# Shared key rests, another query order and earlier turns in a fused attention and FFN kernel

## The chip, the cores and the metric

The kernel runs on one core of a Trainium2 chip. The metric is device time in microseconds (us): the median over several executions. "Span" is the length of one profiled execution, which is some 1.6 to 1.9 us shorter than the time measured around it.

## The reference, cut to what matters

Attention over 8 batches, 12 heads, 448 tokens and 64 dimensions a head; its output, put together over the heads, is the input of a gated FFN.

```python
scores = matmul(q, k.transpose(0, 1, 3, 2)) / sqrt(64)      # q, k, v: (8, 12, 448, 64)
attn_out = matmul(softmax(scores), v)
x = attn_out.transpose(0, 2, 1, 3).reshape(3584, 768)
g = x @ w_gate                                              # 768 x 1536
silu = g * (1 / (1 + exp(-g)))
out = (silu * (x @ w_val)) @ w_out                          # float32, 3584 x 768
```

## The kernel before

Heads are handled in pairs, 48 of them. A pair's scores come in units: a chunk of keys against all 448 queries, both heads side by side in two PSUM banks (one head on rows 0-63 of TensorE, the other on rows 64-127), followed by one exp on ScalarE. Three such "score banks" of two PSUM banks each rotate. The weighted sums need V with a column of ones (so the 65th column gives the softmax's denominator). The result X must be turned, as the FFN needs features on partitions.

The first six pairs are the start. After that the work comes in visits: two or three score units, one pair's weighted sums, then one or two steps of the FFN. The FFN runs in eight blocks of 384 or 512 tokens. A block's gate and value products ("steps") come first, its output products later. Only two small PSUM banks are left for accumulators, value products and output products.

```python
def qk(pr, c):                                  # c: one of 4 chunks of 112 keys
    s = ps_s.tile([128, 2, 512], FP32, tag="s")
    for hx in range(2):
        nc.tensor.matmul(s[:, hx, 0:S], lhsT=t[ts(hx, 64), c * P : c * P + 128],
                         rhs=t[ts(hx, 64), ds(S + (1 - hx) * D, S)], start=True, stop=True)
    nc.scalar.activation(e[:, :, 0:S], s[0:P, :, 0:S], AF.Exp, scale=sm_scale)

def pv_chunk(pr, c):                            # one accumulator bank for both heads
    if c == 0:
        accs[pr] = ps_f.tile([128, 512], FP32, tag="f", name="acc")
    ...                                         # 8 matmuls of 65 columns a chunk

# FFN: gate in a score bank (or a small one), value and output in small banks
gp = ps_s.tile(...) ; group("g", gp) ; tanh on ScalarE
vp = ps_f.tile(...) ; group("v", vp) ; two products on VectorE, into t1 and hts

# loads, by the pair at which they are issued ("g", "v": quarters of the gate and value
# weights, "o": halves of the output weights, "V": values of three pairs)
wq = {
    0: [("qk", 6), ("g", 0), ("v", 0)],
    1: [("V", 2), ("qk", 8, 1), ("g", 1), ("v", 1)],
    3: [("qk", 9, 1), ("qk", 10), ("g", 2), ("v", 2)],
    4: [("g", 3), ("v", 3), ("qk", 12)],
    6: [("V", 3), ("o", 0)],
    7: [("o", 1)],
}
```

q and k of the first 11 pairs are turned by TensorE; later pairs are put in order by GpSimd and turned by a DMA transpose, which I call the key turn below. X of the first 12 pairs is turned by TensorE, that of later pairs by DMA.

The softmax here doesn't subtract the row's maximum and nothing guards it: scores larger than these inputs give would overflow.

## Time and profile before

| | before |
|---|---|
| time, median | 453.26 us |
| span of the profile | 451.7 us |
| first FFN matmul | 29.79 us |
| block 2 starts | 129.86 us |
| last output matmul ends | 446.55 us |
| waits of TensorE after 29.8 us, as listed | 1.2 us |

The prediction, below, shows TensorE's busy shares, a visit of the middle, the start and the tail. Three more views matter for what follows. First the view of waits, TensorE's own, from 30 us on (what waited, for what: us in total, times, longest). There are only four single ones, 1.2 us in all (the two longest shown):

```profile
PE acc L243 <- DVE t L345: 0.4, 1, 0.4
PE rtp L310 <- ACT osb L378: 0.4, 1, 0.4
...
```

Second, from the page: the busy share of the DMA engines in 40 slices of 11.3 us, and the shares of the chain of work that ended last.

```profile
DMA  9999999999969379874749758772503112200033
...
PE 93%; DVE 3%; ACT 2%; issue 1%; DVEq 0%; ACTq 0%
```

### The profile page before, as it was taken

The page shows a single profiled execution, that of the slowest core. Times are in us where ns is not written, and L with a number is a line of the kernel's source. Part 1 is how long each engine was busy: PE and PEld are TensorE (multiplying, and loading weights), DVE is VectorE, ACT ScalarE, POOL GpSimd, SP SyncE. Part 2 cuts the span into 40 slices and gives each one's busy share as a digit, 9 for nine tenths or more (in the row PEclk, how much of TensorE's full clock was granted, in tenths as well). Part 3 has the DMA queues.
Part 4 walks back from the last instruction along what each step waited for, and adds up shares of the span by engine and source line. Part 5 has one row for each costly group of instructions (what it writes and reads, how often), then busy time and mean ns, then how long its engine had stood idle before and what let it go on. Part 6 is the DMA issues. An engine that isn't in the chain of part 4 may idle for free.

```text
span 451.7 us, 9871 instructions
## 1 busy us (share of the span) xinstructions
PE 441.9 (98%) x4024; PEld 247.0 (55%) x4024; DVE 201.6 (45%) x447; ACT 238.8 (53%) x350; POOL 141.8 (31%) x228
## 2 busy tenths in 40 slices
PE   8999999999999999999999999999999999999995
PEld 3655565545455556454555656545455666544563
DVE  3666562456654434455443534353453544055300
ACT  6965666566746465554554546644555462222221
POOL 8755715927642225252313405330100000000000
PEclk9999999999999999999999999999999999999999
DMA  9999999999969379874749758772503112200033
GB/s 142 173 200 201 196 172 174 180 209 119 145 93 133 46 129 124 132 120 71 126 74 120 98 78 143 118 105 68 101 20 68 46 46 57 70 2 0 17 100 95
DMA packets 105101, 48.71 MB, mean 108 GB/s; under 512 B 59744, under 2 KB 101600, under 8 KB 105056
## 3 DMA queue, kind: packets, MB, share of 16 engines
q0 software_dynamic: 43392, 23.37, 41.2%
q1 hardware_dynamic: 61664, 24.71, 28.9%
q8 instruction: 31, 0.51, 0.5%
q14 instruction: 14, 0.11, 0.1%
HBM read 47.19 MB, written 11.01 MB: 129 GB/s over the span
## 4 chain that ended last, share of the span: by engine, by line
PE 93%; DVE 3%; ACT 2%; issue 1%; DVEq 0%; ACTq 0%
PE op L371 24%; PE gp L326 23%; PE vp L326 23%; PE s L217 9%; PE acc L243 9%; PE acc L251 2%; ACT E L225 2%; PE tp L208 1%; PE wp L109 1%; DVE t L345 1%; ACT sg L341 1%; DVE qkT L209 0%; DVE xt L264 0%; PE acc L291 0%; DVE hts L348 0%
## 5 line engine op out<-in xcount | busy, mean ns | idle before, releaser
L225 ACT ACTIVATE E<-s 112x896 f16<-112x896 f32 x192 | 162.1, 919 | 27.5 <-PE s L217 27.4
L326 PE MATMUL gp<-X,wg 128*128 128x384 f16 (+1 forms) x576 | 124.7, 352 | 0.0
L326 PE MATMUL vp<-X,wv 128*128 128x384 f16 (+1 forms) x576 | 124.6, 352 | 0.0
L371 PE MATMUL op<-wo,hts 128*128 128x384 f16 (+1 forms) x684 | 116.1, 323 | 0.0
L345 DVE SCALAR_TENSOR_TENSOR t<-sg,gp 128x384 f32<-128x384 f32 (+1 forms) x96 | 59.7, 621 | 121.8 <-ACT sg L341 121.8
L341 ACT ACTIVATE sg<-gp 128x384 f32<-128x384 f32 (+1 forms) x96 | 52.5, 547 | 84.8 <-PE gp L326 83.6
L371 PEld LDWEIGHTS <-hts 128*128 128x128 f16 x684 | 65.5, 98 | 45.9 <-issue 3.9
L326 PEld LDWEIGHTS <-wv 128*128 128x128 f16 x576 | 56.3, 98 | 52.6
L326 PEld LDWEIGHTS <-wg 128*128 128x128 f16 x576 | 53.1, 97 | 45.6 <-issue 1.1
L378 ACT ACTIVATE osb<-op 128x384 f32<-128x384 f32 (+1 forms) x57 | 27.8, 487 | 92.5 <-PE op L371 92.5
L167 POOL COPY qk<-q 112x512 f16<-112x512 f16 x37 | 22.9, 619 | 144.5 <-DMA qkT<-qk 143.1
L348 DVE SCALAR_TENSOR_TENSOR hts<-t,vp 128x384 f16<-128x384 f32 (+1 forms) x96 | 59.6, 621 | 10.0
L243 PEld LDWEIGHTS <-E 112*128 112x128 f16 x1152 | 46.7, 97 | 18.2 <-issue 17.5
L243 PE MATMUL acc<-vo,E 112*128 112x65 f16 x1152 | 53.0, 193 | 1.3 <-DVE vo L142 0.7
L217 PE MATMUL s<-qkT 64*128 64x448 f16 x384 | 50.6, 355 | 0.2
L251 PE MATMUL acc<-vo,E 112*128 112x65 f16 x384 | 42.9, 193 | 0.0
L262 DVE RECIPROCAL R<-acc 128x7 f32<-128x7 f32 x48 | 9.8, 205 | 70.6 <-PE acc L251 70.5
L129 POOL DMA_DIRECT2D k<-in_k_dram x44 | 29.0, 660 | 9.5 <-DMA wo<-in_moe_w_out_dram 7.8
L129 POOL DMA_DIRECT2D q<-in_q_dram x44 | 29.3, 666 | 5.2 <-PE s L217 2.5
L136 POOL DMA_DIRECT2D vraw<-in_v_dram x42 | 28.0, 666 | 8.4 <-DVE vo L142 7.2
L217 PEld LDWEIGHTS <-qkT 64*128 64x128 f16 x384 | 14.5, 94 | 25.8 <-issue 18.6
L264 DVE TENSOR_TENSOR xt<-acc,R 128x384 f16<-128x384 f32 (+1 forms) x48 | 27.6, 574 | 1.7
(41 smaller groups left out, 148.2 us busy)
## 6 DMA issues: line engine op xcount, KB each, us to landing
q<-in_q_dram POOLq DMA_DIRECT2D x41, 112.0 KB, 4.0
k<-in_k_dram POOLq DMA_DIRECT2D x41, 112.0 KB, 4.6
vraw<-in_v_dram POOLq DMA_DIRECT2D x39, 112.0 KB, 4.6
wg<-in_moe_w_gate_dram POOLq DMA_DIRECT2D x8, 288.0 KB, 10.1
wv<-in_moe_w_val_dram POOLq DMA_DIRECT2D x8, 288.0 KB, 10.2
wo<-in_moe_w_out_dram POOLq DMA_DIRECT2D x2, 1152.0 KB, 22.0
out_dram<-osb SPq DMA_DIRECT2D x8, 288.0 KB, 3.0
out_dram<-osb SPq DMA_DIRECT2D x8, 240.0 KB, 3.1
```

The costliest lines, as they stand in the source:

```text
L129: nc.gpsimd.dma_start(dst[:, ds(h0, 2 * n)], flat.rearrange("h (p c) d -> p h (c d)", c=NC))
L136: nc.gpsimd.dma_start(vraw[:, ds(pr % VS, n)].rearrange("p r h c d -> p (r h) (c d)"), v[b, h : h + 2 * n].rearrange("h (p c) d -> p h (c ...
L217: nc.tensor.matmul(s[:, hx, 0:S], lhsT=t[ts(hx, 64), c * P : c * P + 128], rhs=t[ts(hx, 64), ds(S + (1 - hx) * D, S)], start=True, stop=True,)
L225: nc.scalar.activation(e[:, :, 0:S], s[0:P, :, 0:S], AF.Exp, scale=sm_scale)
L243: nc.tensor.matmul(a7[:, 2 * j + hx], lhsT=e[:, ds(c * EB + 9 * hx + 2 * j, 2)].rearrange("p b x -> p (b x)"), rhs=vo[:, hx, c, 0 : D + 1] ...
L251: nc.tensor.matmul(a7[:, 6], lhsT=e[:, ds(c * EB + 6 + hx, 2)].rearrange("p b x -> p (b x)"), rhs=vo[:, hx, c, 0 : D + 1], start=False, st ...
L326: nc.tensor.matmul(dst[:, 0:n], lhsT=wslice(kind, fb, cb), rhs=X[kk][:, cb, ds(c0, n)], start=(cb == 0), stop=(cb == NCB - 1),)
L341: nc.scalar.activation(sg[:, 0:n], gp[:, 0:n], AF.Tanh, scale=0.5)
L345: nc.vector.scalar_tensor_tensor(t1[:, 0:n], sg[:, 0:n], 1.0, gp[:, 0:n], ALU.add, ALU.mult)
L348: nc.vector.scalar_tensor_tensor(hts[:, fb, 0:n], t1[:, 0:n], 0.5 * HS, vp[:, 0:n], ALU.mult, ALU.mult)
L371: nc.tensor.matmul(op[:, 0:w], lhsT=hts[:, fb, ts(ch, 128)], rhs=wo[oh][:, fb, ds(m0 - oh * OH, w)], start=(fb == 0), stop=(fb == NFB - 1),)
L378: nc.scalar.activation(osb[:, ds(m0, w)], op[:, 0:w], AF.Copy, scale=1.0 / HS)
```

## The change

Its intent: fewer and fuller instructions in attention. Keys come in three chunks of 128 and a rest of 64; the rests of four heads (two pairs) share one score unit on the four 64x64 quarters of the array. That makes 168 units and exps in place of 192. Each head has its own accumulator bank. To make full tiles, queries and keys are loaded in another order (keys and values in two DMAs with a token in common). X of 18 pairs is turned by TensorE, in a score bank. Turns of X go ahead of the next FFN step. The output weights come in four pieces, later than before, and the outputs of block 0 are made in block 1 rather than in block 0.

```diff
-NPE = 11
+NPE = 12
-XPE = 12
+XPE = 18
+START = (
+    "sstssvtsppsppstvsxsvpspppstsppsppsvtsspp"
+    "pvxspsxspppvpstsppxsppsxx"
+)                                  # order of the start: s score, t turn, v copy of V, p sums, x turn of X
...
     def qk(pr, c):
+            ...                    # rest unit: 2 heads x 2 pairs on the four quarters
+            for hx in range(2):
+                for p in (pr, pr + 1):
+                    lo = low(p, hx)
+                    nc.tensor.matmul(
+                        s[ts(1 - lo, 64), hx, 0:S],
+                        lhsT=t[ts(hx, 64), ds(0 if lo else KR * 128 + 64, 64)],
+                        rhs=t[ts(hx, 64), ds(NC * 128, S)], ...
...
-        if c == 0:
-            accs[pr] = ps_f.tile([128, 512], FP32, tag="f", name="acc")
+                accs[pr] = ([fbank(), fbank()], [0, 0])       # a bank a head
...
     def turn_x(pr):
         if pr < XPE:
-            tp = accs[pr] if pr < FIRST else ps_f.tile([128, 512], FP32, tag="f", name="xtp")
+            tp = ps_s.tile([128, 2, 512], FP32, tag="s", name="xtp")[:, 0]
...
-            nc.vector.tensor_copy(dst[:, 0:MQ], tp[:, 0:MQ])
+            nc.vector.tensor_copy(dst, tp[:, 0:S])
-    def turn_rests(b):
-        ...
...                                # output loop: n here overwrites the block's size
-                    c, p0 = divmod((j + D) % S, P)
-                    m = min(P - p0, l0 + 128 - l, (MQ if j < MQ else S) - j)
+                    n = S // NC
+                    c, p0 = divmod(j, n)
+                    m = min(n - p0, l0 + 128 - l)
...
-            1: [("V", 2), ("qk", 8, 1), ("g", 1), ("v", 1)],
-            3: [("qk", 9, 1), ("qk", 10), ("g", 2), ("v", 2)],
-            4: [("g", 3), ("v", 3), ("qk", 12)],
-            6: [("V", 3), ("o", 0)],
-            7: [("o", 1)],
+            1: [("V", 2), ("qk", 8, 1), ("qk", 9, 1), ("g", 1), ("v", 1)],
+            3: [("qk", 10), ("V", 3), ("g", 2), ("v", 2)],
+            4: [("qk", 12), ("g", 3), ("v", 3)],
+            9: [("o", 0), ("o", 1)],
+            11: [("o", 2), ("o", 3)],
...
-            (oq if i == 0 else ffn2_wait).extend(own)
+            ffn2_wait.extend(own)
...
+                for _, p0 in todo:
+                    pv_piece(p0, RU)                          # rest sums straight after the scores
...
+    def run_fv():
+        next(gen)
+        run_turns()                                           # turns of X ahead of later steps
```

## The prediction

> **What bounds the kernel now.** I read the page's busy shares and its row of slices first, then TensorE's order in the steady middle, then the start, then the tail.
>
> The busy shares:
>
> ```profile
> span 451.7 us, 9871 instructions
> PE 441.9 (98%) x4024; PEld 247.0 (55%) x4024; DVE 201.6 (45%) x447; ACT 238.8 (53%) x350; POOL 141.8 (31%) x228
> PE   8999999999999999999999999999999999999995
> ACT  6965666566746465554554546644555462222221
> ```
>
> TensorE (PE) is full in all slices but the first and the last; ScalarE (ACT) has its top value, 9, only in the second. So work that leaves TensorE's order is worth its own length almost everywhere, and work that leaves ScalarE is worth something only in the first 30 us. As ends of matmuls are modelled, I take costs from the start of one group to the start of the next. A visit of the middle (columns: start, length, engine, line, operation, count):
>
> ```profile
> 269.14 0.74 PE L217 MATMUL s<-qkT 64*128 64x448 f16 x6
> 269.82 2.12 PE L371 MATMUL op<-wo,hts 128*128 128x384 f16 x12
> 271.78 1.14 PE L326 MATMUL gp<-X,wg 128*128 128x384 f16 x6
> 272.75 1.14 PE L326 MATMUL vp<-X,wv 128*128 128x384 f16 x6
> 273.82 0.74 PE L217 MATMUL s<-qkT 64*128 64x448 f16 x6
> 274.50 0.36 PE L243 MATMUL acc<-vo,E 112*128 112x65 f16 x6
> ...
> 275.47 0.81 PE L326 MATMUL gp<-X,wg 128*128 128x384 f16 x4
> ```
>
> From the starts: three score units (two heads side by side, 448 columns each) take 274.50 - 273.82 = 0.68 us. A run of two takes 0.48 us (33.78 to 34.26) and a single one 0.29, so a unit is 0.19 us and 0.10 is paid once a run. A group of six FFN matmuls takes 0.97 us before another full-array group (the gate, 271.78 to 272.75) and 1.07 before scores (the value, 272.75 to 273.82). So entering the half-row mode costs 0.10, and leaving it 0.10. A pair's weighted sum, 32 matmuls of 65 columns, takes 275.47 - 274.50 = 0.97 us, 30.5 ns each.
>
> The start, which is ScalarE's: 26 exps run from 6.59 to 29.33, 0.875 us each, nearly unbroken, and the first FFN matmul waits for the sixth pair:
>
> ```profile
> 23.25 6.08 ACT L225 ACTIVATE E<-s 112x896 f16<-112x896 f32 x7 [0.29 <-PE s L217]
> 28.93 0.63 DVE L264 TENSOR_TENSOR xt<-acc,R 128x448 f16<-128x448 f32 x1
> 29.61 0.34 PE L291 MATMUL acc<-ident,xt 128*128 128x128 f16 x3 [0.96 <-DVE xt L264]
> 29.79 1.14 PE L326 MATMUL gp<-X,wg 128*128 128x384 f16 x6
> ```
>
> The tail: TensorE ends near 446.6, one short eviction follows, and then 4.8 us of output transfer and end of program:
>
> ```profile
> 446.59 0.33 ACT L378 ACTIVATE osb<-op 128x192 f32<-128x192 f32 x1 [0.61 <-PE op L371]
> out_dram<-osb SPq DMA_DIRECT2D x10, 192.0 KB, 3.0
> out_dram<-osb SPq DMA_DIRECT2D x12, 48.0 KB, 2.0
> ```
>
> **What the skill says.** The Trainium skill, "TensorEngine Tiling (Array Packing)", section Key Properties: a change of tiling mode drains TensorE, while tiles of one mode load weights and multiply in parallel. The trace agrees on both: 0.10 us a switch, and a score unit of two heads takes 0.19 us, the time of one stream of 448 columns at 2.4 GHz. The same page, Gotcha 1: different row tiles may not write one PSUM bank at a time. That is why the new kernel gives each head its own accumulator; no run yet shows what that costs. "TensorE: Matmul & The Clock Gate", section Wait - 56ns, not 53.3ns?, gives N/2.4 GHz plus about 2.5 ns per matmul: 162.5 ns for 384 columns, and the trace has 0.97/6 = 162 ns.
>
> **The change, part by part.** Counts are from the two built programs, split at the first FFN matmul.
>
> Scores. 448 keys were four chunks of 112; they are now three of 128, and the 64 left over of two heads of two pairs share one unit. Units fall from 192 to 168. The shared unit is four matmuls on the four 64x64 quarters; if all four run together it costs about 0.20 us. After the split: 166 units x 0.187 = 31.0 us before; 124 x 0.187 + 21 x 0.20 = 27.4 after.
>
> Weighted sums. Still 32 matmuls a pair, but 24 use 128 rows and 8 use 64 rows, alternating between the row halves. Pairs of small transposes on different tiles show the likely price: twelve of the present rest-transposes (64 columns) take about 0.21 us without the switch, 17.5 ns each. For 42 pairs after the split: 42 x 0.97 = 40.7 before; 1008 x 30.5 ns + 336 x 17.5 ns = 36.6 after.
>
> Turns. q and k: 3 pairs x 18 x 27.5 ns = 1.5 before; 4 pairs of 8 x 27.5 + 16 x 17.5 ns = 2.0 after (12 pairs are now turned by TensorE, not 11). X: 18 matmuls x 60 ns + 24 rest-transposes x 17.5 = 1.5 before; 36 x 60 + 12 x 30 = 2.5 after (18 pairs, not 12).
>
> Mode switches. 119 before, 132 after: fewer visits (50 against 58), but 21 of the shared units add a step from quarters to halves. At 0.10: 11.9 before, 13.2 after.
>
> FFN. The same columns: 96 x 0.97 + 96 x 1.29 + 56 x 1.95 = 326.1 us in both.
>
> Sum after the split: before 31.0 + 40.7 + 1.5 + 1.5 + 11.9 + 326.1 = 412.7 (the trace has 446.6 - 29.8 = 416.8, so 4 us are waits and small change). After: 27.4 + 36.6 + 2.0 + 2.5 + 13.2 + 326.1 = 407.8. **Gain 4.9 us.**
>
> Start. The sixth pair's sums now need 21 exps, not 24: 3 x 0.875 = 2.6 us earlier. Against it: the first V copy stands ahead of a q/k eviction in VectorE's order, V comes in two issues, and TensorE's own work in the start (some 19 us) is close to ScalarE's 18.4. First FFN matmul near 27.6 instead of 29.8: **gain 2.2**.
>
> Tail. In the output loop a new local n overwrites the block size, so the test for the last tile never holds; the built program has no half-width output matmuls. The last eviction is a full one (0.49 for 0.33), the last transfers are 192 KB (3.0 us) and not 48 KB (2.0): **loss about 1.0**.
>
> New waits. A pair's sums now take both small PSUM banks at once. The output eviction (0.49 us) after the last matmul before a visit must fit under three score units (0.57 us): it just does, but a value bank with its VectorE step (0.56 or 0.69) does not, short by 0.1 to 0.25 us on some 8 visits. In the early visits X is turned in a score bank, freed only by a VectorE copy queued behind two FFN steps: the third score unit of about 5 visits can wait 0.3 to 0.7. Off against waits that vanish (the rest-transposes' 0.6), I put **0.7 to 1 us of net loss**.
>
> ScalarE loses 24 x 0.9 = 22 us and GpSimd, SyncE lose some issues: worth nothing after 30 us. VectorE: two reciprocals and two products (0.2 + an estimated 0.42, twice) replace one each and two rest copies: even.
>
> Total: 453.3 - 4.9 - 2.2 + 1.0 + 0.8 = **448.0 us**, 1.2% faster.
>
> **Rivals.**
> First, the bank waits take all of it. For: only two banks for sums, values and outputs, and the product steps lie on the way to free them. Against: the changed order puts an output step last before most sums. If every one of 50 visits lost 0.15 us more, 7.5 us: about 455.
> Second, everything packs and the waits go: the old trace's unexplained 4 us shrink as well because turns now lead the FFN steps. Then -4.9 - 2.6 + 1.0 - 2.5: about 444, and 442.5 if going from quarters to halves drains nothing (21 x 0.1).
> Third, quarters do not run four at a time (21 x 0.19 = +4.0) or the 64-row sums do not pair (336 x 13 ns = +4.4): 452 each. Against: both row halves (scores) and both column halves (transposes) already run in pairs in this trace.
> Fourth, ScalarE's 22 us count in full: 431. Against: it idles near half of the middle already.
>
> **Range and chances.** The counts are exact; the open terms (waits +-3, packing +4, start +-1) give 443 to 452. Faster by 2% needs under 444.2: only the second rival reaches it (the fourth I don't believe), 0.18. Slower by 2% needs 462: more than any rival, 0.02. Within 2%: 0.80.
>
> **What would show it.** Shared score units spaced 0.2 us (right) or 0.38 (third rival); 24 + 8 sum matmuls in 0.87 us; the first gate matmul near 27.6; TensorE's waits on VectorE and ScalarE under 3 us after it (above 6: first rival); TensorE's last output matmul to the end 5.8 us. The prediction is wrong if the first FFN matmul does not move, or if the sums wait for a bank on most visits.

## More of the kernel before

Third, one line of TensorE's order that will matter: the 57th to 59th score units, the first of pair 14 (start, length, engine, line, operation, count). So the keys of pair 14 are asked for at 84.75 us.

```profile
84.75 0.74 PE L217 MATMUL s<-qkT 64*128 64x448 f16 x6
```

## The result, and the profile after

The changed kernel takes **456.85 us** (median of 4 runs, 456.72 to 456.88), the kernel before 453.26 us (4 runs). Ratios are the mean time of one kernel's fast runs over that of the other's of the same rounds, so they are not quite the ratios of the medians quoted: here 1.0078, with a 95% interval of 1.0061 to 1.0096. That is 0.8% slower where 1.2% faster was predicted, and 4.9 us above the upper end of the range (452).

From the page of the changed kernel:

```profile
span 455.1 us, 10116 instructions
...
PE 440.9 (97%) x4112; PEld 248.8 (55%) x4112; DVE 204.4 (45%) x466; ACT 220.3 (48%) x325; POOL 181.5 (40%) x303
...
PE   8999889999999999999999999999999999999995
...
ACT  5976575445354554455435465454454542222221
```

TensorE does 1.0 us less work in a longer span, and two slices early on (the fifth and sixth show 8) are no longer full: time is lost between 45 and 68 us. ScalarE lost 18.5 us of work (22 predicted), and no time came of it.

Where the time went, as differences between starts in the two traces. The prediction gave its sum by kinds of work; I apportion it here by pairs of sums (14 fall in blocks 0 and 1, 24 in blocks 2 to 5, 4 after): packing is (4.9 + 1.5 of turns) / 42 = 0.152 us a pair, and the turns and the waits lie in blocks 0 and 1.

| stretch | before, us | after, us | change | predicted |
|---|---|---|---|---|
| to the first FFN matmul | 29.79 | 29.78 | 0.0 | -2.2 |
| blocks 0 and 1 | 100.07 | 105.52 | +5.45 | -2.1 + 1.5 + 0.8 = +0.2 |
| blocks 2 to 5 | 211.73 | 209.54 | -2.19 | -3.7 |
| blocks 6 and 7, to the last output matmul | 104.96 | 105.48 | +0.52 | -0.6 |
| tail | 5.17 | 4.76 | -0.41 | +1.0 |
| sum | 451.7 | 455.1 | +3.4 | -5.3 |

**The steady middle packs as planned.** TensorE's order in a visit in which nothing is waited for (same columns as above):

```profile
238.43 0.38 PE L269 MATMUL s<-qkT 64*64 64x448 f16 x4
238.75 0.55 PE L256 MATMUL s<-qkT 64*128 64x448 f16 x4
239.13 0.28 PE L291 MATMUL f<-vo,er 64*128 64x65 f16 x8
239.35 0.91 PE L291 MATMUL f<-vo,E 128*128 128x65 f16 x24
240.09 1.14 PE L379 MATMUL gp<-X,wg 128*128 128x384 f16 x6
```

The shared unit of four matmuls takes 238.75 - 238.43 = 0.32 us with the switch to halves in it, so 0.22 without: the four quarters do run together. The eight rest sums take 239.35 - 239.13 = 0.22 with the switch to the full array (0.10) in it, so about 0.12 without, and the 24 full ones 0.74. In the trace's single records of this visit the eight start in pairs 2 to 4 ns apart, with 26 to 32 ns to the next pair: the two row halves do work at the same time.

**But in most visits the second sum waits for its bank.** Each head now has its own accumulator bank, so the second sum of a pair needs the second small bank at once. A visit just before, with ScalarE's eviction of the output that held the bank:

```profile
229.72 0.49 ACT L431 ACTIVATE osb<-f 128x384 f32<-128x384 f32 x1 [2.65 <-DMA X<-xt]
230.19 0.34 PE L291 MATMUL f<-vo,er 64*128 64x65 f16 x8
230.47 0.90 PE L291 MATMUL f<-vo,E 128*128 128x65 f16 x24
```

The eviction ends at 230.21, the first rest sum started at 230.19, and the second (the other head's) starts only at 230.26. The eight take 0.28 us and not 0.22. Behind a value product it is worse:

```profile
85.43 0.19 PE L291 MATMUL f<-vo,er 64*128 64x65 f16 x1
85.82 0.28 PE L291 MATMUL f<-vo,er 64*128 64x65 f16 x7 [0.20 <-DVE hts L401]
86.03 0.91 PE L291 MATMUL f<-vo,E 128*128 128x65 f16 x24
```

Here they take 86.03 - 85.43 = 0.60. Against 0.22, 27 of the 42 pairs after the first FFN matmul lose 0.05 us or more, and all pairs together lose 5.9 us.

**The early blocks wait.** TensorE's waits from 30 us on:

```profile
PE s L256 <- DVE X L362: 3.1, 5, 0.7
PE f L291 <- DVE hts L401: 1.9, 8, 0.5
PE s L256 <- DMA qkT<-qk: 0.7, 1, 0.7
...
```

With two single ones of 0.5 and 0.4 us, not shown, they come to 6.6 us, against 1.2. The list understates them: it reckons idle time from the modelled end of the matmul before, and leaves out what is under 0.15 us. From start to start, against the same step without a wait, the X copies cost 3.9 us, the second banks 5.9, the keys 0.8 and a turn 0.7: 11.4 us, against about 2.0 in the kernel before. The first row is the score bank in which X was turned and whose copy waits on VectorE behind FFN products; the second is the pair of accumulators waiting for a value bank; the third is new in kind, a wait for a transfer.

**The chain now passes through the DMA engines.** The chain's shares, and further down three of its pieces in order of time (start, length, what):

```profile
PE 79%; DMA 10%; POOL 4%; DVE 2%; issue 2%; ACT 1%; SPq 0%; DVEq 0%; POOLq 0%
```

```profile
62.46 9.56 DMA qkT<-qk
72.02 0.14 issue
72.16 0.36 PE s L256 x2
```

The turned keys of pair 14 were issued at 62.46 and landed 9.56 us later; the median of such turns in this kernel is 4.3. TensorE asks for them at 72 us, and asked for those of the same pair at 84.75 in the kernel before: the 11.9 us of block 0's output products, which stood ahead of them, are now in block 1. The page's row of the DMA engines:

```profile
DMA  9999999999956599557878699945021210300033
```

Eleven slices of nines, as before: the page has the engines at 90% or more all through the first 125 us. In 30 to 72 us they moved 7.84 MB (187 GB/s), and 8.02 MB (191 GB/s) in the same stretch before. So by 72 us both kernels have loaded 13.0 MB, but the changed kernel asks for more by then. In the kernel before, the keys of pair 14 landed at 80.71 us, 4.0 us ahead of their use.

**The start did not move.** Two score units, 8 us apart, and the first FFN matmul:

```profile
10.54 0.56 PE L256 MATMUL s<-qkT 64*128 64x448 f16 x2
...
18.72 0.36 PE L256 MATMUL s<-qkT 64*128 64x448 f16 x2
...
29.78 1.15 PE L379 MATMUL f<-X,wg 128*128 128x384 f16 x6
```

The same unit took 0.56 us at 10.5 and 0.36 at 18.7: TensorE was at its lower clock until about 13.6 us in this execution (until about 6.4 before). The page's row of granted clock shows nines all along and does not show this; lengths of equal instructions do.

**The tail** (engine ACT, then SyncE's queue):

```profile
450.36 0.49 ACT L431 ACTIVATE osb<-f 128x384 f32<-128x384 f32 x1 [1.41 <-PE f L424]
450.88 0.78 SPq L444 DMA_DIRECT2D out_dram<-osb  x2
```

The eviction is a full one, as predicted, but the last tile now has a piece of 112 rows and one of 16. Both are issued by SyncE, as the overwritten block size also switches off the rule that gives a small last piece to ScalarE's queue: SyncE has two issues left after the last eviction. Before, it had six from 445.18 on, and its own issuing (3.69 us for the six) carried into the end.

### The profile page after: what moved, and what is told of

Same layout as the page of the kernel before. It is cut to its first block, busy times and chain, and to the rows that moved or that the text cites.

```text
span 455.1 us, 10116 instructions
## 1 busy us (share of the span) xinstructions
PE 440.9 (97%) x4112; PEld 248.8 (55%) x4112; DVE 204.4 (45%) x466; ACT 220.3 (48%) x325; POOL 181.5 (40%) x303
## 2 busy tenths in 40 slices
DMA packets 101854, 49.17 MB, mean 108 GB/s; under 512 B 56752, under 2 KB 98224, under 8 KB 101808
## 4 chain that ended last, share of the span: by engine, by line
PE 79%; DMA 10%; POOL 4%; DVE 2%; issue 2%; ACT 1%; SPq 0%; DVEq 0%; POOLq 0%
PE f L424 24%; PE f L379 21%; PE gp L379 20%; PE f L291 8%; PE s L256 4%; DMA qkT<-qk 2%; DMA wv<-in_moe_w_val_dram 2%; DMA vraw<-in_v_dram 2%; DMA k<-in_k_dram 2%; DMA q<-in_q_dram 2%; PE s L269 1%; DVE hts L401 1%; DVE t L398 1%; ACT sg L394 1%; POOL q L154 1%
## 5 line engine op out<-in xcount | busy, mean ns | idle before, releaser
L277 ACT ACTIVATE E<-s 128x896 f16<-128x896 f32 x144 | 123.3, 923 | 14.2 <-PE s L256 14.0
L379 PE MATMUL f<-X,wv 128*128 128x384 f16 (+1 forms) x576 | 124.6, 352 | 0.0
L424 PE MATMUL f<-wo,hts 128*128 128x384 f16 x672 | 115.5, 326 | 0.0
L379 PE MATMUL gp<-X,wg 128*128 128x512 f16 (+1 forms) x522 | 113.5, 354 | 0.0
L424 PEld LDWEIGHTS <-hts 128*128 128x128 f16 x672 | 65.1, 98 | 45.9 <-issue 2.2
L431 ACT ACTIVATE osb<-f 128x384 f32<-128x384 f32 x56 | 27.5, 490 | 107.4 <-PE f L424 103.3
L195 POOL COPY qk<-k 128x512 f16<-128x512 f16 x36 | 23.8, 662 | 108.0 <-DMA qkT<-qk 104.9
L401 DVE SCALAR_TENSOR_TENSOR hts<-t,f 128x384 f16<-128x384 f32 (+1 forms) x96 | 59.6, 621 | 10.0
L291 PEld LDWEIGHTS <-E 128*128 128x128 f16 x1152 | 38.4, 98 | 4.3 <-issue 1.6
L291 PE MATMUL f<-vo,E 128*128 128x65 f16 x1008 | 38.0, 193 | 0.0
L330 DVE TENSOR_TENSOR xt<-f,R 128x256 f16<-128x256 f32 x84 | 35.7, 425 | 3.1 <-DMA X<-xt 0.3
```

Source lines behind the costliest of these rows:

```text
L195: nc.gpsimd.tensor_copy(dst.rearrange("p c h d -> p h c d"), src)
L277: nc.scalar.activation(e[:, 0 : 2 * S].rearrange("p (h q) -> p h q", h=2), s[:, :, 0:S], AF.Exp, scale=sm_scale)
L291: nc.tensor.matmul(accs[pr][0][hx][:, ts(j, D + 1)], lhsT=e[rows, ds(hx * S + j * 128, 128)], rhs=Vts[pr % NV][rows, hx, col, 0 : D + 1], ...
L330: nc.vector.tensor_tensor(xt[:, :, hx], a4[:, :, 0:D], r[:].unsqueeze(2).to_broadcast([128, KR + 1, D]), ALU.mult,)
L379: nc.tensor.matmul(dst[:, 0:n], lhsT=wslice(kind, fb, cb), rhs=X[kk][:, cb, ds(c0, n)], start=(cb == 0), stop=(cb == NCB - 1),)
L401: nc.vector.scalar_tensor_tensor(hts[:, fb, 0:n], t1[:, 0:n], 0.5 * HS, vp[:, 0:n], ALU.mult, ALU.mult)
```

## The experiments

Eighteen kernels were run, told here as four sets. Each run was timed against the kernel before on the same chip; 453.3 to 453.7 us is the median of that kernel in all sets. Where a text uses letters for theories, they hold for its own set only; I name the theories in words. "Faster than the changed kernel" needs care across sets: the changed kernel itself has the ratio 1.0078 [1.0061, 1.0096].

### Set 1: clock in the start, X's copies, X's turns

Theory: the slow clock in the start ate the start's gain, and the waits for the X copies ate the rest. Rival: either can be taken away without a gain.

**warm**: the changed kernel with four filler matmuls in its start again.

```diff
-    "sstssvtsppsppstvsxsvpspppstsppsppsvtsspp"
+    "ssdtdsddsvtsppsppstvsxsvpspppstsppsppsvtsspp"     # d: one filler matmul
```

> The changed kernel with four of the removed filler matmuls (128x512, full array) put back among its first turns and scores. Theory A (the array runs at half clock until 13.6 us because the start is now almost all 64-row and 64-column work, and the exps starve for TensorE at 8.9 to 13.8): the clock record begins by about 7 to 10 us, a single score unit takes 0.36 and not 0.56 at 8 to 13 us, the first FFN matmul moves from 29.8 to about 28.2, and the kernel from 456.9 to about 455.2. Rival B (the start waits for V transfers and VectorE's queue): the first FFN matmul stays at 29.8 and the fillers cost up to 0.9 us: 456.9 to 457.8.

Measured: 457.22 us (456.18 to 458.47), ratio 1.0082 [1.0063, 1.0100]. The clock came up at 10.7 us rather than 13.6, the first FFN matmul at 29.65, and nothing was gained in time; a key turn was waited for 0.95 us.

**cold**: the kernel before without its four fillers.

```diff
             if u == 1:
-                dummy(1)
                 turn()
-                dummy(1)
-            elif u == 3:
-                dummy(2)
```

> The kernel before with its four filler matmuls among the first turns and scores taken away. Theory A: it now stays at half clock well past 6.6 us, its exps get gaps like those of the changed kernel, first FFN matmul later by 0.5 to 2 us and the time 453.8 to 455.3. Rival B: no change or 0.5 us faster (453.3 to 452.7), since fillers only cost time.

Measured: 453.18 us, ratio 0.9990 [0.9978, 1.0003]; clock up at 6.6 us, first FFN matmul at 29.47. The fillers do not matter: nothing is gained with them or lost without. What the runs below do show is that when the clock comes up and when the first FFN matmul comes go together in the changed kernels: up by 3.9 to 5.6 us in those without extra fillers, matmul at 27.2 to 27.9; up at 10.6 to 13.6, matmul at 29.7 to 30.7.

**xact**: from pair 6 on, X is copied out of the score bank by ScalarE, which is idle half of the time, instead of VectorE.

```diff
-            nc.vector.tensor_copy(dst, tp[:, 0:S])
+            if pr < FIRST:
+                nc.vector.tensor_copy(dst, tp[:, 0:S])
+            else:
+                nc.scalar.activation(dst, tp[:, 0:S], AF.Copy)
```

> The changed kernel with the copy of the turned X (pairs 6 to 17) out of its score bank done by ScalarE, not by VectorE behind the two FFN products. Theory A (the third score unit of five early visits waits 0.58 to 0.70 us, 3.1 in all, for that VectorE copy): those waits fall below 0.25 each and the kernel gains 2 to 3 us: about 454.3. Rival B (the early visits are bound by transfers of keys and queries, or by ScalarE itself): another wait takes their place, 456 to 457.5.

Measured: 456.68 us (456.22 to 459.73), ratio 1.0088 [1.0062, 1.0113]. The waits for X fell from 3.9 to 1.2 us (from start to start), and the first FFN matmul came at 27.62, as predicted for the change. The time did not fall. TensorE's order shows why:

```profile
58.65 0.55 PE L256 MATMUL s<-qkT 64*128 64x448 f16 x4 [2.62 <-DMA qkT<-qk]
...
60.57 2.11 PE L382 MATMUL gp<-X,wg 128*128 128x384 f16 x6
```

TensorE now waits 2.62 us for turned keys (3.8 in two waits, for 0.7 before), and the gate group after that takes 2.11 us, not 1.14: after the wait the clock was halved for 3.4 us. Block 2 starts at 134.8, for 135.3. The slow stretch is not the whole reason: an execution at clock 0.999, so without one, took 456.60 us. The Trainium skill, "TensorE: Matmul & The Clock Gate", section Part 1: The HAM clock gate, says that the gate looks at a free-running window of some 3.4 us and halves the clock after an idle one. The length of the slow stretch agrees; the wait ahead of it was shorter than a window.

**xpe12**: X of 12 pairs turned by TensorE, not of 18.

```diff
-XPE = 18
+XPE = 12
```

> The changed kernel with pairs 12 to 17 of X turned by DMA again, as in the kernel before. Theory A (six more pairs cost TensorE 24 matmuls of 58 ns): 1.2 to 1.5 us faster, about 455.5. Rival B (they were moved to TensorE because the DMA turns come too late for the next FFN block): waits on DMA appear at the second block, time 456.5 to 459.

Measured: 456.69 us, ratio 1.0070 [1.0054, 1.0087]. The turns of X after the split fell from 2.83 to 1.65 us and block 1 from 55.92 to 54.95, but the time cannot be told from that of the changed kernel.

### Set 2: the price of the rest sums, the tail, and the sum of the fixes

**unpaired**: the eight rest sums of a pair head by head, so that no two neighbours use different row halves. The theory is the prediction's: pairing saves 8 x (30.5 - 17.5) = 104 ns a pair. Rival: pairing saves little.

```diff
+        order = [(j, hx) for j in range(KR + 1) for hx in heads]
+        if c == RU and pr >= FIRST:
+            order = [(j, hx) for hx in heads for j in range(KR + 1)]
```

> The changed kernel with the eight rest sums of a pair issued head by head (four on one row half, then four on the other), so that neighbours use the same row half. Theory A (alternating halves run in pairs, 17.5 ns each against 30.5 alone): 42 pairs x 8 x 13 ns = 4.4 us slower, less up to 2 us because the second head's bank is now needed 0.12 us later: 459 to 461. Rival B (they do not run in pairs, 0.14 us was never gained): no slower, 456 to 457.

Measured: 457.40 us (456.00 to 458.99), ratio 1.0087 [1.0064, 1.0110]. A steady block takes 50.54 us for 50.50. That doesn't show that pairing is worth little, because the edit did not undo it. Where both banks are free (238.71, for one), the sum that waits for the second bank, fifth in the program's order, starts 8 ns after the first, and the eight lie 111 ns apart from first to last start, against 96 in the changed kernel: the two heads still overlap. Where the second bank is late by more than 0.1 us, the first four run alone, about 30 ns apart, and the four of the other head follow when the bank is free, so the eight take what they took anyway (0.60 us behind a value product, in both kernels). What four of one row half alone cost, 30 ns each, is the prediction's price of an unpaired sum.

**restlast**: the rest sums after the full ones and not between scores and full sums; that adds a change of mode each way.

```diff
     def pv(pr):
         ...
+        pv_piece(pr, RU)
...
-                for _, p0 in todo:
-                    pv_piece(p0, RU)
```

> The changed kernel with the rest sums of a pair after its full sums and not between scores and full sums: per pair two more changes of tiling mode (scores to full, full to halves, halves to full in place of halves to full alone), and the second bank is needed 0.4 us later. Theory A (a change of mode costs 0.10 us): 42 x 0.2 = 8.4 us of switches, less about 2.5 us of bank waits that vanish: 462 to 463.5. Rival B (switches cost nothing by themselves, the bank waits do): 454 to 455.

Measured: 460.87 us (459.02 to 461.42, 5 runs), ratio 1.0157 [1.0136, 1.0178]. A steady block is 0.71 us longer, 0.12 a pair. TensorE's order in a visit:

```profile
233.22 0.91 PE L291 MATMUL f<-vo,E 128*128 128x65 f16 x24
234.06 0.29 PE L291 MATMUL f<-vo,er 64*128 64x65 f16 x8
234.29 1.47 PE L380 MATMUL gp<-X,wg 128*128 128x512 f16 x6
```

The full sums take 234.06 - 233.22 = 0.84 us before the rests, and 0.74 before an FFN group: that is the 0.10 of a switch again. The waits for the second bank fell from 5.9 to 0.6 us, and this is the run that shows what they cost. From the first FFN matmul to the last output matmul it takes 7.0 us more than the changed kernel: 42 x 0.20 = 8.4 of switches, less 5.3 of bank waits, plus 2.2 of key waits (its first FFN matmul came 2.45 us earlier, at 27.33) and 1.7 of half clock is 7.0. So the sizes of the switches in the prediction hold, and the bank waits are real; this way of avoiding them costs more than they do.

**tail**: the local variable renamed, so that the last tile is split as before.

```diff
-                    n = S // NC
-                    c, p0 = divmod(j, n)
-                    m = min(n - p0, l0 + 128 - l)
+                    c, p0 = divmod(j, P)
+                    m = min(P - p0, l0 + 128 - l)
```

> The changed kernel with the block size no longer overwritten, so that the last tile's output is again written in a half and two quarters. Prediction's view: the split saves about 1.0 us: 455.9. Rival, from the two traces (4.7 us from the last output matmul to the end without the split, 5.1 with it): 456.5 to 457.3, no gain.

Measured: 455.64 us (454.76 to 455.93), ratio 1.0041 [1.0024, 1.0058]. The tail is 3.70 us, for 4.76. The lost split costs 1.06 us, as predicted (1.0); that it is now shorter than in the kernel before (5.17) goes with the pieces of 16 and 112 rows, of which the small ones are issued by ScalarE's queue (before_tail, below, tests that).

**combo**: warm, xact and xpe12 together.

> Fillers back in the start, X copied by ScalarE, pairs 12 to 17 of X turned by DMA, all three together. If the three costs are separate and additive (1.7, 2.5, 1.3): 451.4, 0.4% faster than the kernel before. If they hide one another: 453 to 456.

Measured: 455.82 us, ratio 1.0050 [1.0036, 1.0064]; expected if the parts added up: 451.4. The key wait was 1.75 us and block 2 started at 133.9, with the first FFN matmul at 30.66. Here stands the observation that no theory about banks explains. In the seven kernels with the changed kernel's order of loads and its steady packing (the changed kernel, warm, xact, xpe12, unpaired, tail, combo), the first FFN matmul came between 27.4 and 30.7, and block 2 started between 133.9 and 135.4 whatever it was. In unpaired, for one, the first FFN matmul came 2.36 us earlier than in the changed kernel, TensorE waited 2.8 us for keys and not 0.7, and block 2 started 0.5 us earlier. Why can be read at one place. In these seven and in restlast, the keys of pair 14 landed between 71.5 and 72.2 us, and its first score unit started between 71.6 and 72.3, whatever had been gained or lost ahead of it; block 2 then started 63.1 to 63.2 us later in five of them, 62.0 in the two with X of 12 pairs, and 65.1 in restlast. So what is gained ahead of pair 14 is given back to the wait for its keys.

### Set 3: other orders of loads

Theory: if keys are turned ahead of the last weights, and the output weights, first used at 103 us, come later, the waits vanish and the start's and the X copies' gain is kept. Rival: all of it is needed in time, and the wait only goes elsewhere. The Trainium skill, "Trainium Kernel Development and Optimization", section Key Constraints, says that DMAs from SyncE, ScalarE and GpSimd run on the same 16 engines and interleave; if so, another queue would not free a late transfer (no run tried it). A key turn that took 9.56 us while weights were loaded, for a median of 4.3, fits.

**loads**, **loads_x** (with xact), **loads_all** (with xact, tail, xpe12 and fillers):

```diff
-            3: [("qk", 10), ("V", 3), ("g", 2), ("v", 2)],
-            4: [("qk", 12), ("g", 3), ("v", 3)],
-            9: [("o", 0), ("o", 1)],
-            11: [("o", 2), ("o", 3)],
+            3: [("qk", 10), ("V", 3), ("qk", 12), ("g", 2), ("v", 2)],
+            4: [("g", 3), ("v", 3)],
+            13: [("o", 0)],
+            14: [("o", 1)],
+            15: [("o", 2)],
+            16: [("o", 3)],
```

> The changed kernel with only its issue order of transfers altered: keys and queries of pairs 12 and 13 ahead of the last two quarters of the gate and value weights, and the four pieces of the output weights at pairs 13 to 16 instead of 9 and 11. Theory C (the first 72 us are set by the transfers: the turned keys of pairs 12 and 14 land at 57 to 58.5 and 70 to 72 us, whatever TensorE gains before is waited away there): the waits on the turned keys go (0.7 to 3.8 us before, by how early the clock came up), 454 to 456 with a late clock, 452.5 to 454 with an early one. Rival (those waits are only where slack shows, the bound is elsewhere): 456 to 457.5, unchanged.

> The same order of transfers, and X of pairs 6 to 17 copied by ScalarE. Theory C: now the 3.1 us of waits on VectorE's copy, which bought nothing alone (456.7 for 456.9), are really gained: 2 to 3 us less than the run with the new order alone, 451 to 453. Rival (ScalarE's own queue costs as much): equal to the run with the new order alone, within 0.7 us.

> New order of transfers, X copied by ScalarE, pairs 12 to 17 of X turned by DMA, the last tile split again (alone it gave 1.2), fillers back in the start. If the gains add once the transfers no longer bind (3.0 with the order and X, 1.2 tail, 1.2 turns, 0 to 2 start): 448 to 451, faster than the kernel before by 0.5 to 1.2%. If the transfers still bind: 453 to 456.

Measured: loads 459.87 us (455.91 to 461.21), ratio 1.0124 [1.0090, 1.0159]; loads_x 462.52, 1.0209 [1.0189, 1.0230]; loads_all 465.75, 1.0269 [1.0245, 1.0293]. The expectations failed. There is no key wait left in loads, and block 0 shortens from 49.60 to 49.08 us (46.93 in loads_x, where the X copies' gain is really there), but the wait is now for the output weights:

```profile
PE f L424 <- DMA wo<-in_moe_w_out_dram: 5.2, 1, 5.2
```

In loads_all it is 12.0 us in two waits, and TensorE ran 13.65 us at its lower clock. I had put the output weights too late. The profiled execution of loads is its slowest, 461.21 us at clock 0.992; two of its six, at 0.998 and 0.999, took 455.91 and 456.80.

**loads2**, **loads2_x** (with xact), **loads2_all** (with all fixes), **loads2_nofill** (the same without fillers): the pieces of the output weights at pairs 10, 11, 12 and 13.

Relative to loads, with lines joined:

```diff
-            13: [("o", 0)],   14: [("o", 1)],   15: [("o", 2)],   16: [("o", 3)],
+            10: [("o", 0)],   11: [("o", 1)],   12: [("o", 2)],   13: [("o", 3)],
```

> The order of transfers as in the last call (keys and queries of pairs 12 and 13 ahead of the last two quarters of gate and value weights), but the four pieces of the output weights at pairs 10 to 13, which is where that run's transfers landed in 2.4 to 4 us, and not at 13 to 16, where the first output step waited 5.2 us for them. Theory C (the first 80 us are set by which transfer comes when): no wait of TensorE on a transfer over 0.3 us after 29.8, first FFN block in 47 to 49.5 us and second in 55.9; 454.5 to 456 with a late clock, 452.5 to 454 with an early one. Rival (any order only moves the wait, since the bytes themselves are too many): a wait of 1 us or more on keys or output weights stays, 456 or more.

> The same with X of pairs 6 to 17 copied by ScalarE. Theory C: the first FFN block in 47 us, the second in 55.9, 2 to 2.5 us less than the run beside it with VectorE's copy: 451 to 453.5. Rival: equal to it within 0.7.

> The same with X by ScalarE, pairs 12 to 17 of X turned by DMA, the last tile split again and fillers in the start. If the gains add: 448.5 to 451, faster than the kernel before by 0.5 to 1.1%. If transfers bind again (six more pairs turned by DMA): 453 to 456.

> As the run beside it, without the five extra fillers. Theory A on the clock (fillers bring the full clock earlier): 0.5 to 2 us slower than with them. Rival (when the clock comes up is the luck[...], fillers only cost): equal or up to 0.8 us faster.

Measured: loads2 461.24 us, ratio 1.0144 [1.0114, 1.0174]; loads2_x 459.66, 1.0122 [1.0101, 1.0143]; loads2_all 458.09, 1.0089 [1.0069, 1.0109]; loads2_nofill 458.01, 1.0091 [1.0069, 1.0113]. No wait for the output weights, but one for keys, ending at 78 to 82 us: 6.5 us in loads2, and 3.0, 5.75 and 6.1 us in the other three (the profiled execution of loads2 is its slowest, 463.54 us). The rival holds: each of these orders left 3 to 12 us of waits for transfers somewhere between 78 and 113 us. The fillers again make no difference.

### Set 4: fewer bytes, and the tail of the kernel before

**skipv**: the values of pairs 12 to 23 are not loaded at all, so the result is wrong. Theory: bytes are what binds; 1.57 MB less (47.60 in place of 49.17 MB over the span) would end the key waits. Rival: what binds is the order, or the time that a turn takes behind large transfers. **skipv_x** has xact too.

```diff
-                if 12 <= pr + 3 < NPAIR:
+                if 24 <= pr + 3 < NPAIR:
                     load_v(pr + 3)
```

> The changed kernel with the V transfers of pairs 12 to 23 left out; those pairs use the V that lies in the buffer, so the result is wrong on purpose, while every instruction of TensorE, VectorE and ScalarE stays. It takes 12 x 229 KB out of the transfers between about 48 and 110 us and changes nothing else. Theory C' (the first blocks are bound by the bytes that must arrive, in whatever order): the turned keys of pairs 14 and later land 3 us or more earlier, the wait on them at 72 us goes; 455.5 to 456.5 with a late clock (0.7 us was waited), 453 to 455 with an early one. Rival (bank waits alone are the bound): 456.7 to 457, no change.

> The same V transfers left out (wrong result on purpose) and X of pairs 6 to 17 copied by ScalarE. With all transfers that copy bought nothing (456.7). Theory C': with fewer bytes it buys 2 to 3 us against the run beside it: 452 to 454.5. Rival: no more than 0.7 us, 455 or more.

Measured: skipv 456.71 us, ratio 1.0073 [1.0056, 1.0090]; skipv_x 457.22, 1.0083 [1.0067, 1.0100]. No gain, and key waits of 3.2 and 3.1 us in the profiled executions, the slowest of their runs (458.31 and 458.39). The keys of pair 14 landed at 70.1 us, 1.9 earlier and not 3 or more, and pair 16's were then waited for. But the test is not clean: GpSimd, rid of the value loads, issued the output weights earlier (at 55.0 us, not 58.9), and key turns still took 9 to 13 us to land behind them (one from 64.62 to 77.47). So bytes alone are not shown to bind; the order of the transfers is not shown to, either.

**before_tail**: the kernel before, with the second piece of rows of the last outputs issued from ScalarE's queue. Theory: SyncE's issuing is what lengthened the tail before.

```diff
-                    eng = nc.scalar if last and m < 64 else nc.sync
+                    eng = nc.scalar if last and p0 == 0 else nc.sync
```

> The kernel before with the second of the two row pieces of each last output issued from ScalarE's queue and not behind the first on SyncE's (six issues take 3.69 us there, two of them after the last eviction). If the issue queue makes the difference between its 5.2 us from the last output matmul to the end and the 3.7 us of the changed kernel with the split: 452.0 to 452.6, the fastest of all. If the transfers themselves do: 453.2 to 453.7.

Measured: **452.57 us** (452.28 to 452.76), ratio 0.9978 [0.9965, 0.9992], the fastest kernel, 0.2% ahead of the kernel before. The tail fell from 5.17 to 4.23 us. SyncE's last issues, first in the kernel before, then here:

```profile
445.18 3.69 SPq L390 DMA_DIRECT2D out_dram<-osb  x6
```

```profile
445.16 2.42 SPq L390 DMA_DIRECT2D out_dram<-osb  x3
```

Three issues fewer stand in SyncE's queue and it is done 1.29 us earlier.

## Why the prediction was wrong

**Right: the packing.** A shared unit takes 0.22 us (0.20 was put), a switch 0.10, and the eight rest sums about 0.12 without the switch (8 x 17.5 ns = 0.14 was put). Both halves of the third rival are refuted: quarters run together, and the 64-row sums pair. Blocks 2 to 5 gained 2.19 us where 3.7 was due, but 2.19 us of waits for the second bank stand in them; without these they would have gained 4.4. From the first FFN matmul to the last output matmul, TensorE took 416.8 us before and 420.5 after: the waits grew by 9.4 us (2.0 to 11.4), so the rest shrank by some 5.6, where 4.9 was predicted.

**Failed: "New waits … 0.7 to 1 us of net loss".** This is the step that turned a gain into a loss: the net is 9.4 us. The waits were named rightly and mis-sized. "A value bank with its VectorE step … does not [fit], short by 0.1 to 0.25 us on some 8 visits": behind a value product the second bank came 0.33 to 0.65 us late in ten visits, 4.1 us. "The output eviction (0.49 us) … must fit under three score units (0.57 us): it just does": it does not. The eviction starts 0.11 us after the score units (229.72 for 229.61), ends at 230.21 and comes 0.06 too late, and so in 15 visits (0.05 to 0.11 us each), 1.0 us. With two other visits (0.2 and 0.64) 27 of 42 pairs lost 0.05 us or more. In all that is 5.9 us. The five X copies cost 0.74 to 0.86 us each, 3.9 in all (predicted 0.3 to 0.7). The prediction's own list already came to more than it wrote: 5 x 0.5 + 8 x 0.18 - 0.6 = 3.3 us. And one of its signs of being wrong came true: the sums wait for a bank on most visits.

**Failed: "Start … gain 2.2".** It was 0.0 in the profiled run, where the clock came up at 13.6 us. The 2.2 did occur where it came up early (27.3 to 27.6 us in xact, unpaired, restlast and loads), so the 21 exps are rightly counted. But it was worth no more than 0.5 us even then: the keys of pair 14 were waited for instead.

**The rivals.** The first, "the bank waits take all of it", is right for the changed kernel: it put 0.15 us on each of 50 visits, 7.5 us and a time of about 455, and the runs show 0.14 us on each of 42 pairs, 5.9 us, besides the X copies. Its mark (over 6 us of waits) was met. What none of the four asked is whether data would be there, and that is why the repairs did not pay. xact removed 2.8 us of bank waits and started 2.2 us earlier, and block 2 started only 0.5 earlier, because the keys of pair 14 land near 72 us in every kernel with this order of transfers. In the kernel as changed this limit cost only the 0.8 us of its own key wait. The other orders (loads, loads2) and the loads without V (skipv) all had waits for transfers too, at 58 to 113 us.

**Mis-signed: the tail ("loss about 1.0").** The 1.0 us of the lost split is right (tail: 1.06). The step missed is that the row order also decides how the last tile falls apart into pieces and who issues them: 4.76 - 1.06 = 3.70 against 5.17, which is 1.5 us. On the kernel before, a change of queue alone saved 0.94 of it (before_tail); the rest goes with the sizes of the pieces and was not run. The changed kernel's tail is short for another reason: unsplit, it has two last issues and not six.

**What stays open.** Three things. First, some 5.0 of the 5.9 us of waits for the second bank lie after 72 us, where the keys of pair 14 no longer set the time; no run freed that bank earlier without adding switches, so what that would gain is not shown. Second, why the kernel before, with the same rate of transfer, has no waits for keys. Its keys of pair 14 are asked for some 13 us later (84.75, against 72.16 less a wait of 0.69), after the 11.9 us of block 0's outputs, and had landed 4.0 us before; that the move of these outputs into block 1 is the cause was argued from the two traces and not run. Third, whether bytes, the order in the queue, or the time of a key turn beside large transfers binds; skipv could not tell.

## What to carry to other kernels

When TensorE is full nearly everywhere, a change that makes its early part shorter also makes it ask for data earlier: before counting such a gain, compare when each tile is needed after the change with when it can land, in the stretch where the DMA engines are busy throughout. Add up the waits that you list, count times size, before you write down their total; and where a buffer must come free under a stretch of work, count from the start of that work to the release, with the lag before the freeing instruction starts: 0.49 us under 0.57 did not fit here. Measure waits from start to start, since many small ones stay under a list's threshold. When a variant is meant to undo something, check in its trace that it did (unpaired did not). And look at which queue issues the last outputs: in the kernel before, that was worth 0.94 us.

## What the Trainium skill lacked or had wrong

- "TensorEngine Tiling (Array Packing)" says that a change of mode drains TensorE but gives no time: here it is 0.10 us, in the kernel before, in the changed one and in restlast.
- The same page gives no size for what the accumulator banks of separate row tiles can cost: here a second bank a pair cost 5.9 us of waits over 42 pairs.
- "TensorE: Matmul & The Clock Gate" speaks of idle windows of some 3.4 us: in xact a single wait of 2.62 us led to half clock for 3.4 us. And in the start, with TensorE at work on small pieces, the full clock came only at 3.9 to 13.6 us, and differed between executions of kernels that are nearly the same.
- No page that I read says how long a DMA transpose takes to land beside large loads: 4.3 us in the median of the changed kernel, 9.56 for the one in the chain, and 12.9 for the longest in skipv.
